# One bank of a first network layer set ahead of the second step's off-diagonal products

## The chip, the cores and the metric

The kernel runs on one core of a Trainium2 chip. The metric is the device time of one execution in microseconds (us). A core has a matrix engine (PE, with its weight loads shown apart as PEld), a vector engine (DVE), a scalar engine (ACT), a general engine (POOL) and a queue engine (SP) that here only issues DMAs. Each engine works through its own instructions in order and waits for the others by semaphores.

## What is computed

Two blocks in a row. The first is a linear attention with a forget gate; the second is a network with a per-feature leaky activation:

```python
# q, k, v, f_logit: (B=4, H=8, S=768, D=48), float32
f = 1.0 / (1.0 + np.exp(-f_logit))
for t in range(S):
    state = f[:, :, t, :, None] * state + np.einsum('bhd,bhe->bhde', k[:, :, t], v[:, :, t])
    y[:, :, t] = np.einsum('bhd,bhde->bhe', q[:, :, t], state)
x = y.transpose(0, 2, 1, 3).reshape(B * S, H * D)        # 3072 tokens x 384
h = x @ w_in                                              # 384 x 2048
g = np.maximum(h, 0.0) + alpha * np.minimum(h, 0.0)
return g @ w_out                                          # 2048 x 384
```

## The kernel before

**Steps.** The sequence is cut into 6 chunks of 128 tokens, and the batch into 2 pairs of sequences. One step is one chunk of one pair (256 tokens); there are 12 steps, and the two pairs alternate. The first two steps belong to the first chunk (c = 0), where there is no state yet to start from, and they take some paths of their own.

**What a step does.** Four generators write the instructions of a step; each `yield` ends a piece.
- `prepare` (letters P and Q) loads q, k, f and v, applies the sigmoid, and builds on DVE and ACT the scaled copies of q and k (`qd`, `us`, `q3`, `kh`, `ks`, `k4`) from scans of f. Its sixth and last piece copies parts of `q3` into the attention matrix `A` (L407, ACT).
- `carry` (O), first piece: PE computes the off-diagonal products `off` (L432, and for c = 0 also L442), ACT copies them into `ad` (L446) and `A` (L450); for c = 0 PE also transposes `ks` into `pk` (L459), and ACT copies that to `ksn` (L462). Second piece: PE multiplies `ksn` with v into `pd` (L472), which feeds the state kept beside v in `vs`.
- `attend` (S): for each of two sequences PE computes `raw` (L508) and `qu` (L523), and DVE moves the allowed entries into `ad` (L514, L545 for c = 0 or L529 else). Then ACT copies `ad` into `A` (L551), PE computes `py` from `vs` and `A` (L562), and the result is copied (L571) and turned into `xT`, the network's input: on PE in the first step (`xt`, L580, copied by L582), by DMAs in the others.
- `network` (n): in each of its first eight pieces PE fills one PSUM bank `ph` with two column tiles of x @ w_in (L606: 6 products of 128x128 by 256, which the trace shows as 12 MATMUL), ACT forms `neg` (L611), and DVE forms `gate` in two operations (L613). Then follows the second layer: in the first step 32 products into `po` (L626) over the whole of w_out, later a scheme with sums and fewer products (L645).

**Weights.** The weights arrive as 64-bit words and are converted by hand. For each of 8 pieces of w_in and 8 of w_out, ACT runs three operations (L201, L203, L204; letter a for w_in, b for w_out), and DVE a `lead` (L214) and a `both` (L219; letters w and v). The raw words have four buffers and are loaded by SP; the operations between ACT and DVE have three. A piece of w_in holds just the columns of one bank of the first step. Letter W closes this stage and forms differences of blocks of w_out on DVE (L706).

**PSUM.** `raw`, `qu`, `off`, `pk`, `pd` and `py` share one pool of two pairs of banks; `ph`, `xt` and `po` share a pool of four single banks. A tile waits until the earlier one in its place has been read.

**Order.** The order of PE, DVE and ACT is the order of the program, which is written out by hand as a string of letters for each step: a letter with a number takes that many pieces of that generator. In the string of step n, P, O and S stand for the pieces of step n, lower-case n for the network of step n - 1, and Q for `prepare` of step n + 1. The first four steps have strings of their own (`first`, L712), the others share `usual` (L718). So the string of the second step, which the change touches, holds the network of the first step, the `carry` and `attend` of the second, and the first five pieces of `prepare` of the third.

Of the kernel before, what the change touches and what calls it, by code (L numbers as in the profile page):

```python
# [31 lines left out]
def kernel(  # L32
# [39 lines left out]
    W = U * HP * C  # L72
# [66 lines left out]
    for m in range(1, NB):  # L139
        lo = UO[m] + (4 if m == 1 else 0)  # L140
        n = NB - m
# [4 lines left out]
    for half in range(2):  # L146
        for m in range(1, NQ):
            n = NQ - m
# [540 lines left out]
    def halves_of_w_out():  # L689
# [21 lines left out]
    steps = [(bp, c) for c in range(NC) for bp in range(B // U)]  # L711
    first = (  # L712
        "P5 a w P a2 O w S w a w a2 S Q S O S w Q2 S Q2 S w",
        "a2 w b w O w n2 b2 v S P v2 n2 S b v Q n b n O S2 v n b v n Q2 b v Q b n S v2 W Q W S n2 W n W",
        "n S P n2 S n W n O Q n3 O S Q n S Q n Q S2 Q n3",
        "S n3 P S Q S n O n O n4 Q S Q S Q n S Q n Q n2",
    )
# [81 lines left out]
```

## Time and profile before

| what | value |
|---|---|
| median of 3 runs | 625.14 us (624.67 to 626.03) |
| the profiled execution | 626.43 us, its span 624.6 us |
| mean granted clock of PE in the span | 0.995 |
| PE busy | 589.2 us, 94% of the span |
| DVE busy | 503.4 us, 81% |
| ACT busy | 260.5 us, 42% |
| POOL busy | 62.9 us, 10% |

The span runs from the first to the last instruction of the profiled execution; times within the trace count from its start. PE is busy 3.66 us from 40 to 45 us, 3.01 in the next five, 1.65 from 50 to 55 us, 4.53 from 55 to 60 us, and in nearly every window after it throughout. ACT is busy for most of the time up to 97 us and far less later. A timeline line gives start, duration, engine, source line, operation, output from inputs, shape and count; behind it in brackets stands the idle time of the engine before the group and what ended it. "issue" stands for a wait whose end the profile cannot name.

### The profile page before, as it was taken

The page shows a single profiled execution, that of the slowest core. Times are in us where ns is not written, and L with a number is a line of the kernel's source. Part 1 is how long each engine was busy: PE and PEld are TensorE (multiplying, and loading weights), DVE is VectorE, ACT ScalarE, POOL GpSimd, SP SyncE. Part 2 cuts the span into 40 slices and gives each one's busy share as a digit, 9 for nine tenths or more (in the row PEclk, how much of TensorE's full clock was granted, in tenths as well). Part 3 has the DMA queues.
Part 4 walks back from the last instruction along what each step waited for, and adds up shares of the span by engine and source line. Part 5 has one row for each costly group of instructions (what it writes and reads, how often), then busy time and mean ns, then how long its engine had stood idle before and what let it go on. Part 6 is the DMA issues. An engine that isn't in the chain of part 4 may idle for free.

```text
span 624.6 us, 19118 instructions
## 1 busy us (share of the span) xinstructions
PE 589.2 (94%) x8220; PEld 525.9 (84%) x8220; DVE 503.4 (81%) x1013; ACT 260.5 (42%) x482; POOL 62.9 (10%) x119
## 2 busy tenths in 40 slices
PE   3457999999999999999999999999999999999997
PEld 3346876789889889889889889889889889889997
DVE  7589989899799798889889888888888889762261
ACT  5797992261443252342343343243244244223110
POOL 9120010001001001001001001001001000000000
PEclk9998999899999999999999999999999999999999
DMA  9866513213314313413413313413314301201000
GB/s 298 278 225 196 200 41 93 75 35 86 87 36 90 82 35 86 87 35 85 87 35 85 75 49 85 83 38 87 73 49 85 68 22 26 53 3 26 26 0 26
DMA packets 68116, 50.43 MB, mean 81 GB/s; under 512 B 47168, under 2 KB 60608, under 8 KB 68032
## 3 DMA queue, kind: packets, MB, share of 16 engines
q1 hardware_dynamic: 56656, 25.01, 15.8%
q0 software_dynamic: 6864, 22.35, 12.6%
q10 hardware_dynamic: 4512, 1.85, 1.6%
q8 instruction: 65, 1.06, 0.8%
q14 instruction: 19, 0.16, 0.1%
HBM read 36.21 MB, written 4.72 MB: 66 GB/s over the span
## 4 chain that ended last, share of the span: by engine, by line
PE 60%; DVE 18%; ACT 16%; issue 4%; DMA 1%; ACTq 1%; DVEq 0%
PE ph L606 24%; PE pc L645 9%; PE pa L645 6%; PE pe L645 5%; PE pd L645 5%; ACT A L551 4%; ACT us L302 3%; DVE gate L613 3%; PE qu L523 3%; DVE S L687 3%; PE raw L508 3%; DVE qd L275 2%; PE py L562 2%; ACT neg L611 2%; PE pb L645 1%
## 5 line engine op out<-in xcount | busy, mean ns | idle before, releaser
L606 PE MATMUL ph<-xT,w_in_sb 128*128 128x256 f32 x1152 | 262.7, 385 | 0.0
L606 PEld LDWEIGHTS ph<-xT,w_in_sb 128*128 128x128 f32 x1152 | 216.8, 191 | 33.1 <-issue 2.6
L611 ACT ACTIVATE neg<-ph 128x512 f32<-128x512 f32 x96 | 57.1, 596 | 197.2 <-PE ph L606 156.1
L613 DVE SCALAR_TENSOR_TENSOR gate<-neg,om,ph 128x256 f32<-128x256 f32 x192 | 82.2, 478 | 50.3 <-ACT neg L611 50.2
L645 PE MATMUL pc<-t,S 128*128 128x192 f32 x352 | 61.7, 329 | 0.0
L645 PE MATMUL pa<-w_out_sb,gate 128*128 128x192 f32 x352 | 61.0, 327 | 0.0
L645 PEld LDWEIGHTS pa<-w_out_sb,gate 128*128 128x128 f32 x352 | 58.0, 190 | 0.6
L645 PEld LDWEIGHTS pc<-t,S 128*128 128x128 f32 x352 | 57.3, 190 | 0.6
L514 DVE COPY_PREDICATED ad<-mraw,raw 128x256 f32<-128x256 int32 (+1 forms) x96 | 42.4, 441 | 8.3 <-PE raw L508 5.8
L529 DVE COPY_PREDICATED ad<-mquad,qu 128x224 f32<-128x224 int32 (+6 forms) x140 | 41.9, 300 | 6.2
L407 ACT COPY A<-q 48x512 f32<-48x512 f32 x44 | 27.2, 617 | 37.4 <-DVE q L356 37.0
L551 ACT COPY A<-ad 32x256 f32<-32x256 f32 x96 | 38.6, 402 | 1.4
L318 DVE TENSOR_TENSOR us<-us,fs 128x768 f32<-128x768 f32 (+5 forms) x60 | 36.7, 612 | 0.0
L663 ACT COPY o<-pa 128x192 f32<-128x192 f32 x11 | 3.5, 318 | 75.3 <-PE pa L645 72.3
L562 PEld LDWEIGHTS py<-A,vs 128*64 128x64 f32 x768 | 25.7, 145 | 7.8 <-ACT A L551 3.3
L562 PE MATMUL py<-A,vs 128*64 128x64 f32 x768 | 28.7, 232 | 3.4 <-ACT A L551 1.4
L687 DVE TENSOR_TENSOR S<-gate 128x512 f32<-128x512 f32 x44 | 30.3, 688 | 0.8
L645 PE MATMUL pb<-t,gate 128*128 128x192 f32 x176 | 30.4, 326 | 0.0
L645 PE MATMUL pe<-w_out_sb,S 128*128 128x192 f32 x176 | 30.4, 326 | 0.0
L645 PE MATMUL pd<-w_out_sb,S 128*128 128x192 f32 x176 | 30.4, 326 | 0.0
L508 PEld LDWEIGHTS raw<-qd,k 48*32 48x32 f32 x1536 | 18.3, 109 | 14.0 <-issue 8.4
L508 PE MATMUL raw<-qd,k 48*32 48x80 f32 x1536 | 23.3, 243 | 6.8 <-ACT A L450 5.2
(109 smaller groups left out, 754.6 us busy)
## 6 DMA issues: line engine op xcount, KB each, us to landing
w_out_raw<-in_w_out SPq DMA_DIRECT2D x8, 767.8 KB, 4.4
w_in_raw<-in_w_in SPq DMA_DIRECT2D x8, 767.2 KB, 9.8
q<-in_qT POOLq DMA_DIRECT2D x11, 512.0 KB, 4.4
f<-in_fT POOLq DMA_DIRECT2D x11, 512.0 KB, 4.2
k<-in_kT POOLq DMA_DIRECT2D x11, 512.0 KB, 4.6
out<-o SPq DMA_DIRECT2D x24, 192.0 KB, 2.8
vs<-in_v POOLq DMA_DIRECT2D x22, 192.0 KB, 4.6
ksn<-kt SPq DMA_DIRECT2D x80, 32.0 KB, 2.0
```

Source lines behind the costliest of these rows:

```text
L318: nc.vector.tensor_tensor(us[:, :, UO[m]:UO[m] + 4 * n].rearrange("p g (i r) -> p g i r", r=4), us[:, :, skip:skip + 4 * n].rearrange("p g ...
L407: nc.scalar.copy(A[halves(cc)[1], :, par * HP:(par + 1) * HP, CH * cc:CH * (cc + 1)], q3[rows(par)].rearrange("p (u h c) s t -> p u h c (s ...
L508: nc.tensor.matmul(raw[DB * j:DB * (j + 1), par, hp * C:hp * C + QW], lhsT=k[r_, g * DB:(g + 1) * DB], rhs=qd[r_, g], start=True, stop=True)
L514: nc.vector.copy_predicated(adu[:, :, :, d:4], mraw[:, d, :, d:4].bitcast(I32).unsqueeze(1).broadcast_to((128, H, NB, n)), rv[:, :, QO[d]: ...
L529: nc.vector.copy_predicated(ad[:, u, :, :, 4 * m:DB], mquad[:, lo:lo + n].bitcast(I32).unsqueeze(1).unsqueeze(1).broadcast_to((128, 2, HP, ...
L551: nc.scalar.copy(A[s_, u, :, s_], ad[s_, u].rearrange("p r h t -> p (r h) t"))
L562: nc.tensor.matmul(py[64 * par:64 * par + 64, u, o:o + CH], lhsT=vs[bp][:, cc, u, hd * D:hd * D + 64], rhs=A[:, u, par * HP + hp, CH * cc: ...
L606: nc.tensor.matmul(ph[:, j * T:(j + 1) * T], lhsT=w_in_sb[:, kt, m * 128:(m + 1) * 128], rhs=xT[:, kt], start=(kt == 0 and j == 0), stop=( ...
L611: nc.scalar.activation(neg, phv, AF.Relu, scale=-1.0)
L613: nc.vector.scalar_tensor_tensor(gate[:, m % NH, m // NH], neg[:, j], om[:, m:m + 1], phv[:, j], ALU.mult, ALU.add)
L645: nc.tensor.matmul(to[:, 0:DH], lhsT=of(f), rhs=by(f), start=(f == 0 and not more), stop=(f == NH - 1), skip_group_check=True)
L687: nc.vector.tensor_tensor(to, x_, y_, op)
```

## The change

In the string of the second step, one of the two network pieces that stood together moves ahead of the O (the first piece of `carry` of the second step), behind the second w. Everything else stays.

```diff
     first = (
         "P5 a w P a2 O w S w a w a2 S Q S O S w Q2 S Q2 S w",
-        "a2 w b w O w n2 b2 v S P v2 n2 S b v Q n b n O S2 v n b v n Q2 b v Q b n S v2 W Q W S n2 W n W",
+        "a2 w b w n O w n b2 v S P v2 n2 S b v Q n b n O S2 v n b v n Q2 b v Q b n S v2 W Q W S n2 W n W",
```

On PE the first bank's 12 MATMUL now follow the `xt` products of the first step and precede `off` and `pk` of the second. On ACT its `neg` stands after the conversion of the first w_out piece and ahead of the copies L446, L450 and L462. On DVE its two `gate` operations stand ahead of the last `both` of w_in. The second bank keeps its place.

## The prediction

> **What bounds the kernel now.** I read the page first (PE busy 94% of the span), then windows of 10 us: PE is busy 9.7 us or more of every ten from 120 us to 620 us, so from there on PE sets the pace, and what is won before 120 us should arrive at the end. The change sits at 50 to 65 us. There, the timeline of PE (start, duration, engine, line; idle time before it in brackets):
>
> ```profile
> 46.97 2.83 PE L580 MATMUL xt<-y,dense 128*128 128x256 f32 x12 [1.79 <-ACT y L571]
> 51.59 0.75 PE L432 MATMUL off<-q,kh 48*32 48x32 f32 x64 [1.80 <-DVE q L356]
> 53.13 0.90 PE L442 MATMUL off<-us 48*32 48x16 f32 x86 [0.79 <-DVE us L392]
> 55.45 0.65 PE L442 MATMUL off<-us 48*32 48x16 f32 x42 [1.42 <-issue]
> 56.12 1.97 PE L459 MATMUL pk<-ident,ks 128*128 128x128 f32 x8
> 57.88 5.70 PE L606 MATMUL ph<-xT,w_in_sb 128*128 128x256 f32 x24
> 63.51 0.92 PE L508 MATMUL raw<-qd,k 48*32 48x80 f32 x64
> ```
>
> The reader is to see holes of 1.80, 0.79 and 1.42 us before 56 us, and the two banks (24 matmuls) only after them. The timeline of ACT shows who waits for the second bank:
>
> ```profile
> 58.48 0.92 ACT L204 ACTIVATE w_out_sb<-w_out_raw 128x768 int32<-128x768 uint32 x1
> 59.30 0.39 ACT L446 COPY ad<-off 128x128 f32<-128x128 f32 x2
> 59.60 1.26 ACT L450 COPY A<-off 32x256 f32<-32x256 f32 x4
> 60.89 1.07 ACT L462 COPY ksn<-pk 128x512 f32<-128x512 f32 x2
> 61.85 0.62 ACT L611 ACTIVATE neg<-ph 128x512 f32<-128x512 f32 x1
> 63.61 0.60 ACT L611 ACTIVATE neg<-ph 128x512 f32<-128x512 f32 x1 [1.15 <-PE ph L606]
> 64.11 1.01 ACT L201 ACTIVATE w_out_pos<-w_out_raw,bias 128x768 int16<-128x768 int16 x1
> ```
>
> After that 1.15 us ACT works without a gap over 0.3 us until 96.5 us, on the weights above all, so its start at 64.11 sets its end. DVE hangs on it, and PE on DVE:
>
> ```profile
> 87.02 0.56 DVE L214 TENSOR_TENSOR w_out_lead<-w_out_pos,w_out_neg 128x768 bf16<-128x768 bf16 x1 [1.02 <-ACT w_out_neg L203]
> ...
> 115.73 2.29 DVE L529 COPY_PREDICATED ad<-mquad,qu 128x224 f32<-128x224 int32 x7
> ```
> ```profile
> 118.17 1.07 PE L523 MATMUL qu<-us,k 48*32 48x112 f32 x64 [1.19 <-DVE ad L529]
> ```
>
> From 87.02 DVE has no gap up to 118.03, and the chain of waits runs the same way: ACT to 96, DVE from 100 to 118, then PE. In 56 to 116 us PE has almost no gap either, but it does not end last.
>
> **The change, part by part.** Nothing is removed or added: the bank's 12 matmuls and 12 weight loads, one `neg` on ACT and two `gate` operations on DVE move. The bank issues no DMA, and nothing on SP or POOL stands in another order.
>
> *PE.* A matmul of a bank takes 5.45/24 = 0.227 us (the undisturbed 24 at 65.08), a bank 2.73. The bank now follows `xt`, whose last product ends at 49.80; the last third needs the copy of `xT` at 49.83 + 0.37 = 50.20. If the first eight run before that it ends at 52.5, if all wait for it at 52.9. I take 52.7. What is queued behind it is `off`, which could go at 51.45 (DVE L356): it comes 1.1 us later. Its second group starts near 53.4 instead of 53.13. The hole before 55.45 has no named releaser: either it ends at a fixed time (then `pk` starts at 56.1 as before), or it moves with `off` (at most 1.1 us, `pk` at 57.2). With `pk` at its 1.97 the second bank ends at 60.9 to 62.0. Those who wait for `off` and `pk` are the copies of ACT, which reach them at 59.8 and 61.4; cover 2.5 us at the least, and without it the loss would be the 1.1.
>
> *ACT.* The moved `neg` stands now after the weights' conversion that ends at 59.3 and before the eight copies. Its step is 64.11 - 63.61 = 0.50 us. The bank was done 6 us earlier, so it does not wait. The copies slide by 0.50 and end at 62.35; the second `neg` follows at 62.35, with its bank done 0.4 to 1.5 us before. So the next conversion starts at 62.35 + 0.50 = 62.85 instead of 64.11: **1.26 us earlier**. The bounds are 0.9 (the later end of the bank, and its wake-up) and 1.35 (the short gap before the fourth `neg`, near 70.9, goes too).
>
> *What the sliding copies hold up.* `raw` takes the bank pair of `off`, free when L450 ends: 60.86 + 0.50 = 61.4; `qu` that of `pk`, 62.4. So PE stands idle up to 0.5 us before `raw` and a moment before `qu`, and the third and fourth banks start at 63.2 instead of 65.08: PE is 1.8 us ahead from there on. The fourth ends at 68.7; ACT wants it at 70.9 - 1.26 = 69.6. Cover 0.9 us.
>
> *DVE.* Its order gets two `gate`s (0.87) ahead of the last `both` of w_in: `neg` is ready at 59.9, DVE comes at 60.4, no wait. That `both` is 0.87 later; its piece is first read by the eighth bank near 81 us, so 18 us hide it. The second pair of `gate`s starts at 63.0 instead of 64.24, 1.24 earlier, and the rest of DVE follows in step with ACT (its idle 1.31 and 1.02 us at 84 and 87 are waits for ACT, which come earlier too). Loads: the weights' DMAs are released by ACT's conversions and move with them; the next steps' by PE and DVE.
>
> *Sum.* ACT, then DVE, then `qu` come 1.26 us earlier, at 116.9; PE is there 1.8 earlier and its wait grows from 1.19 to about 1.7. PE alone would give more, but DVE ends last. From 120 us PE carries 1.26 to the end. The profiled execution has 626.43 us (span 624.6, and 1.8 around it); 626.43 - 1.26 = 625.17. It lies 1.29 above the median of the runs, so I carry over the difference: 625.14 - 1.26 = **623.9**.
>
> *The clock.* Windows of 2 us (length, PE busy, granted clock, DMA, GB/s) show it halved twice in the span, both times after a stretch with holes and small products:
>
> ```profile
> 56.00:58.00 2.00, 1.99 (x16) 0.50 0.88 258
> ...
> 120.00:122.00 2.00, 2.00 (x5) 0.51 0.39 160
> 122.00:124.00 2.00, 2.00 (x7) 0.64 0.03 8
> ```
>
> The 24 matmuls at 119.17 took 7.40 us instead of 5.45: 1.95 lost on the path of the end. The change moves such stretches: it fills the first, opens one at 60.9 to 63.2, and makes the one before 119 longer (3.1 us from `raw` to `ph`, then about 3.7). What the clock does there the trace of before cannot say; bounded by the same row: 1.95 spared to 1.95 added. I take 0, since the second stretch was there and was charged already, and keep both ends.
>
> The Trainium skill ("TensorE: Matmul & The Clock Gate", Part 1 and "Why this matters for your kernels") says that the gate judges free-running windows of about 3.4 us and asks for no PE gap over some 3 us. Here a gap of 1.19 us among small products was enough for 3.4 us at half clock, so the measurement decides on the length of the gap. By the page's rule neither stretch would be charged and the sum would stay 1.26; by this trace the longer stretch speaks against the change, and free-running windows would make the charge vary from one execution to the next.
>
> **The rivals.**
> 1. *The clock spares time too.* With the half-clock stretch starting where PE still waits at 115 to 117, part of the 1.95 falls on idle time. For: `ph` now starts 1.26 earlier against the same window. Against: the stretch is longer. Price up to 1.95, I take half: 625.14 - 1.26 - 0.95 = 622.9.
> 2. *The gain is swallowed.* The new hole at 60.9 to 63.2 halves the clock for the third and fourth banks. They lose up to 1.95, the fourth ends at 70.65, and ACT waits for it where it stood before (70.5): 625.1, no change. For: 2.3 us of small products and waits there. Against: full banks on both sides.
> 3. *Slower: the longer wait before `qu` near 116 costs a half clock that the runs of the median did not have.* Price 1.95 against the gain of 1.26: 625.14 + 0.7 = 625.8; if the bank's gain goes as in rival 2 as well, 627.1. It decides when the stretch without full products passes from 3.1 us, charged perhaps only in some runs (the profiled one stands 1.29 above the median), to one that is always charged. Against: the profile has the charge already.
> 4. *The change does nothing*, if the bank could not start at 50 because its weights are not there. The first piece of w_in was finished at 24.6 and the bank's PSUM slot is long free: I give it nothing of its own.
>
> **How the numbers follow.** The forecast has 0.58, with 623.3 to 624.5 as its own range; rival 1 0.16, rival 2 0.12, rival 3 0.14. What a measurement can tell from no change is about 0.2%, 1.25 us, and the forecast stands just on that edge: I give half of it to faster (0.29) and half to within. Faster: 0.29 + 0.14 from rival 1 = 0.43. Slower: 0.09 from rival 3. The rest, 0.48, is within. The range must take in most of rivals 1 and 3: 622.3 to 626.0.
>
> **What would show it.** Right: a bank of 12 matmuls at 50 us ahead of `off`; no wait of ACT L611 before 63; the conversion after it near 62.9; the `qu` that waits for L529 near 116.9. Wrong: ACT idle before the first `off` copy at 59.8 (then `off` came too late); ACT waiting for the fourth bank near 70 (rival 2); DVE waiting between 87 and 118 for something else than ACT; a granted clock below 1 in more windows than these two (rival 3). If ACT's conversions come 1.2 us earlier and the end does not, the claim that PE only carries on from 120 us is wrong.

## The result and the profile after

The changed kernel takes 623.47 us (median of 20 runs, 622.71 to 626.52) against 625.12 us before (20 runs, 623.40 to 626.81): ratio 0.9977, 95% interval 0.9969 to 0.9986, or 1.65 us between the medians. The forecast was 623.9. The profiled executions stand at 625.07 (span 623.3) and 626.43: 1.36 apart, and both lie above their medians.

The timeline of PE in the changed kernel, the same stretch as before (start, duration, engine, line; idle time ahead of it in brackets):

```profile
46.82 4.72 PE L580 MATMUL xt<-y,dense 128*128 128x256 f32 x12 [1.68 <-ACT y L571]
51.37 2.75 PE L606 MATMUL ph<-xT,w_in_sb 128*128 128x256 f32 x12
54.06 0.76 PE L432 MATMUL off<-q,kh 48*32 48x32 f32 x64
...
56.23 1.09 PE L459 MATMUL pk<-ident,ks 128*128 128x128 f32 x8
57.16 2.76 PE L606 MATMUL ph<-xT,w_in_sb 128*128 128x256 f32 x12
61.72 0.92 PE L508 MATMUL raw<-qd,k 48*32 48x80 f32 x64 [1.80 <-ACT A L450]
```

The first bank stands ahead of `off`, `pk` starts about where it did (56.12 before), and the second bank ends at 59.9 instead of 63.6: one bank less stands there, 2.7 us, and `pk` took 1.09 us here, 1.97 before, where the granted clock read 0.50. PE then waits for ACT's copies. The timeline of ACT:

```profile
59.62 0.60 ACT L611 ACTIVATE neg<-ph 128x512 f32<-128x512 f32 x1
60.10 0.44 ACT L446 COPY ad<-off 128x128 f32<-128x128 f32 x2
...
62.65 0.61 ACT L611 ACTIVATE neg<-ph 128x512 f32<-128x512 f32 x1
63.14 1.01 ACT L201 ACTIVATE w_out_pos<-w_out_raw,bias 128x768 int16<-128x768 int16 x1
```

No wait before the second `neg`; the conversions behind it start 0.97 us earlier than in the first trace (64.11). And the end of the stretch, from the timelines of DVE and PE:

```profile
86.05 0.56 DVE L214 TENSOR_TENSOR w_out_lead<-w_out_pos,w_out_neg 128x768 bf16<-128x768 bf16 x1 [1.02 <-ACT w_out_neg L203]
...
114.77 2.30 DVE L529 COPY_PREDICATED ad<-mquad,qu 128x224 f32<-128x224 int32 x7
```
```profile
117.21 1.07 PE L523 MATMUL qu<-us,k 48*32 48x112 f32 x64 [1.36 <-DVE ad L529]
118.21 7.23 PE L606 MATMUL ph<-xT,w_in_sb 128*128 128x256 f32 x24
```

Everything is 0.96 us earlier, in step: 86.05 against 87.02, 114.77 against 115.73, 117.21 against 118.17. The half clock behind `qu` is there as before (7.23, before 7.40). What is new is `xt`: the same 12 matmuls took 4.72 us, before 2.83. So this one trace differs from the first by more than the change, and the experiments had to part the two.

### The profile page after: what moved, and what is told of

The parts are those of the page before. It is cut to its first block, busy times and chain, and to the rows that moved or that the text cites. A ratio compares the mean times of both kernels' runs of the same rounds, so it can differ in the third digit from the quotient of the medians.

```text
span 623.3 us, 19117 instructions
## 1 busy us (share of the span) xinstructions
PE 589.7 (95%) x8220; PEld 526.0 (84%) x8220; DVE 503.7 (81%) x1013; ACT 260.4 (42%) x482; POOL 62.7 (10%) x119
## 3 DMA queue, kind: packets, MB, share of 16 engines
HBM read 36.21 MB, written 4.72 MB: 66 GB/s over the span
## 4 chain that ended last, share of the span: by engine, by line
PE 58%; DVE 15%; ACT 12%; issue 3%; ACTq 0%; DMA 0%; DVEq 0%
PE ph L606 23%; PE pc L645 9%; PE pa L645 6%; PE pe L645 5%; PE pd L645 5%; ACT A L551 4%; DVE gate L613 3%; ACT us L302 3%; DVE S L687 3%; PE qu L523 3%; PE raw L508 2%; DVE qd L275 2%; PE py L562 2%; ACT neg L611 2%; PE pb L645 1%
## 5 line engine op out<-in xcount | busy, mean ns | idle before, releaser
L529 DVE COPY_PREDICATED ad<-mquad,qu 128x224 f32<-128x224 int32 (+6 forms) x140 | 42.0, 300 | 6.2
```

What stands on the lines that cost most here:

```text
L529: nc.vector.copy_predicated(ad[:, u, :, :, 4 * m:DB], mquad[:, lo:lo + n].bitcast(I32).unsqueeze(1).unsqueeze(1).broadcast_to((128, 2, HP, ...
```

## The experiments

The experiments were timed beside runs of the kernel before on the same chip, whose medians were 625.07 (e1 to e4, 35 runs), 625.29 (e5 to e8, 33) and 625.15 (e9 to e12, 21).

**e1, ACT's order alone.** The banks stay where they were; a conversion stands between the two `neg`s.

```diff
-        "a2 w b w O w n2 b2 v S P v2 ...
+        "a2 w b w O w n b n b v S P v2 ...
```

> The old order on PE: both banks stay behind off and pk. Only ACT is reordered: the next weight conversion (2.7 us) stands between the two negs, so that ACT no longer waits for the second bank. The theory (the gain is ACT's 1.15 us wait, handed on by DVE) expects the conversions behind it about 1.2 us earlier and about the gain of the change: 623.5 to 624.0 against 625.1. The rival that PE's work in its hole is what pays (2.7 us of matmuls taken out of the busy stretch) expects no gain, 625.1. The rival that the spared half clock pays expects 625.1 as well.

Measured: 624.72 us, ratio 0.9989 (0.9978 to 0.9999). Most of the gain is missing. The conversion did start at 62.42, but then the timelines of PE and ACT show:

```profile
56.97 7.03 PE L606 MATMUL ph<-xT,w_in_sb 128*128 128x256 f32 x24
...
65.36 5.45 PE L606 MATMUL ph<-xT,w_in_sb 128*128 128x256 f32 x24
```
```profile
69.25 0.59 ACT L611 ACTIVATE neg<-ph 128x512 f32<-128x512 f32 x1
70.90 0.60 ACT L611 ACTIVATE neg<-ph 128x512 f32<-128x512 f32 x1 [1.07 <-issue]
```

That last line is the `neg` of the fourth bank. PE ran `raw`, `qu` and these banks as late as before, and finished the fourth at 65.36 + 5.45 = 70.81; the 1.07 us end there, though the profile names no releaser. DVE L529 starts at 115.73, exactly as before. So ACT's wait was not the only thing that held the path; PE stood just behind it. PE was late by the clock here: the first two banks took 7.03 us, with the granted clock at 0.50 from 58 to 60 us. At the 5.45 us of the next two banks, the fourth would have ended near 69.2, ahead of ACT at about 69.7; this is an estimate, and no such execution of e1 was traced.

**e2, the hole filled without moving work.** The first bank is computed in the hole and again at its old place.

```diff
         for f in range(NH):
             ...
+            if plain and f == 0:
+                yield
+                for kt in range(NK):
+                    ...                      # the same products once more
-        "a2 w b w O w n2 b2 v S P v2 ...
+        "a2 w b w n O w n2 b2 v S P v2 ...
```

> The order of before, but the first bank is computed twice: once in the hole ahead of off, and again at its old place. PE has the hole filled and no work less afterwards. The rival of the clock expects the whole gain, 623.5. The rival of PE's work expects none, 625.1 or a little more. The theory of ACT's wait expects only what an earlier end of the second bank gives: off 1.1 us later, pk and the banks at full clock if the fill keeps it up, so the wait before the second neg shrinks from 1.15 to between 0.2 and 1.1 us: 624.2 to 625.1, and the shift of the conversions must equal the shift of the end.

Measured: 624.90 us, ratio 0.9991 (0.9979 to 1.0003), which is not told apart from no change. The runs fall into two groups, 623.08 to 623.62 (4 of 11) and 624.53 to 625.18 (7). The trace is one of the first group, with the full clock granted from 52 us to 120 us: there `pk` took 1.09, the conversions started at 62.76 and `qu` at 116.84. In lines, of PE and of ACT:

```profile
55.83 1.09 PE L459 MATMUL pk<-ident,ks 128*128 128x128 f32 x8
```
```profile
62.76 1.03 ACT L201 ACTIVATE w_out_pos<-w_out_raw,bias 128x768 int16<-128x768 int16 x1
```

So with 2.7 us more for PE to do, a full clock behind the hole alone was worth as much as the change, where it came about. This was the first sign that the clock on this stretch matters.

**e3, more work for ACT in the changed kernel.**

```diff
-            nc.scalar.activation(pos, top, AF.Relu, bias=bias[:, 0:1], scale=8.0)
+            for _ in range(3 if name == "w_out" and n == 1 else 1):
+                nc.scalar.activation(pos, top, AF.Relu, bias=bias[:, 0:1], scale=8.0)
```

> The changed kernel, with the first operation of the second w_out piece's conversion run three times instead of once: about 2 x 0.9 = 1.8 us more on ACT, right after the second neg; PE and DVE have the same work as in the changed kernel. The theory of ACT expects the whole 1.8 us at the end: 623.5 + 1.8 = 625.3, the gain gone. The rivals of PE's work and of the clock expect the gain to stay, 623.5, since ACT is busy 42% of the span.

Measured: 626.22 us, ratio 1.0022 (1.0010 to 1.0033). The edit adds a line, so L201 is L202 here:

```profile
62.81 3.06 ACT L202 ACTIVATE w_out_pos<-w_out_raw,bias 128x768 int16<-128x768 int16 x3
```

The three operations take 3.06 us, 2.05 more than the one of the changed kernel's first trace, and start 0.33 earlier (63.14 there), so ACT should be 1.72 us later behind them. `qu` starts at 118.92, 1.71 us later: the added work arrives there whole, though ACT is busy 42% of the span. The medians differ by more, 2.75 us; 5 of the 12 runs lie above 627, with a mean granted clock of 0.994 or 0.995. Why those are more frequent, and why even the three at 1.0 lie at 625.92 to 626.23, was not followed up.

**e4, one lead earlier on DVE.** The last `w` of the first string stands ahead of L482 and L486, to take away ACT's wait at 55.3.

```diff
-        "... O S w Q2 S Q2 S w",
+        "... O S w Q2 S Q2 w S",
```

> The changed kernel, and in the string of the first step the last w stands one piece earlier, ahead of the two state updates of DVE (L482, L486, 2.1 us). ACT waits there for this lead before the first w_out conversion (1.36 us before the change, 0 in the profile of the changed kernel, where xt was slow). The theory of ACT expects up to 1.2 us more where xt runs at full clock, and 0.3 to 0.8 where it does not: 622.3 to 623.2. The rival of PE's work expects no gain or a loss up to 1.5 us, since pk waits for L486, which comes 1.5 us later: 623.5 to 625.

Measured: 624.71 us, ratio 0.9994 (0.9983 to 1.0006): a loss of 1.2 us against the changed kernel, where the theory of ACT expected a gain and the rival up to this loss. The timeline of PE shows where it begins:

```profile
57.54 1.65 PE L459 MATMUL pk<-ident,ks 128*128 128x128 f32 x8 [1.35 <-DVE vs L486]
58.99 3.92 PE L606 MATMUL ph<-xT,w_in_sb 128*128 128x256 f32 x12
```

`pk` waits for L486, which was moved back. PE stands idle for 1.35 us more, the clock halves behind it, and the second bank ends at 62.9 instead of 59.9 (61.1 in e7 below, where the clock halves too). In this trace `qu` starts at 117.52, only 0.31 us later than in the changed kernel's first trace and 0.76 later than in e7, so it shows a part of the loss of the medians. This also answers what the prediction left open: `pk` starts near 56 in either order because L486 ends there (at 56.06 before, at 55.89 in the changed kernel's first trace), so the bank in the hole cost `pk` next to nothing.

**e5 and e6, the later wait filled in both kernels.** In the third step one bank is set between `raw` and `qu` of the second sequence, where PE waits for L529.

```diff
+            if (bp, c) == steps[2] and u == 1:
+                yield                        # between raw and qu
...
-        "n S P n2 S n W n O Q n3 ...
+        "n S P n2 S n S W n O Q n3 ...
```

> The changed kernel, and in the third step one network bank stands between raw and qu of the second sequence, where PE otherwise waits 1.2 to 1.4 us for DVE near 116 us and the clock then halves in many executions. If that wait and its half clock are on the path, the wait (1.36 us) is filled with work that has to be done anyway, and the 1.8 us of half clock behind it vanish: 621.5 to 622.5 against 623.5. If DVE is the bound after 118 us, nothing is won: 623.3.

> The kernel of before with the same edit in the third step. The difference between this and the changed kernel with the edit is what the change is worth where no half clock behind that wait can be charged. If the change's gain is the earlier handing on through ACT, DVE and PE, about 1.0 us of difference is left. If the gain is that fewer executions are charged the half clock near 119 us, the difference shrinks to 0.3 us or less, as the few executions without half-clock windows suggest (before 623.5 to 624.1, changed 623.2 to 623.7).

Measured: 623.26 us with the change (e5, ratio 0.9967, 0.9956 to 0.9979), 624.49 without it (e6, 0.9994, 0.9985 to 1.0004). The difference stays, 1.23 us, with neither the wait nor the half clock behind it in either trace (PE goes from `raw` to the bank to `qu` without a gap). As e6 expected for the theory of the path, about 1 us of difference is left; so the change does not live on fewer half clocks near 119 us. The edit itself brought little, 623.26 where 621.5 to 622.5 was expected if the wait were on the path: in e5 `off` of the third step comes at 122.38, against 123.51 in e7 below, yet the two traces stand at 623.46 and 623.40. In the new order the gates and sums of the bank stand ahead of the second L529 on DVE, which ends at 126.0 instead of 122.4; that DVE then holds the path is the likely reason, and was not tried by itself.

**e7, e9 and e10, more traces of the two kernels.** Unchanged code, other executions.

> The changed kernel once more, for a second trace and more times. The trace of the changed kernel has the half clock at 118 to 123 us and 625.07 us; most executions lie near 623.4. If the half clock near 119 us is what parts them, an execution near 623.4 shows 24 matmuls of ph behind the waiting qu in 5.45 us and not 7.23, and the same times up to there within 0.4 us.

> The kernel of before once more, for a second trace in another position of the clock's windows. Mechanism: the conversions after the second neg near 64.0 whatever the clock does to xt, since ACT waits there for the second bank; qu behind L529 near 118.1. The 24 matmuls behind it 5.5 to 5.8 us where the time is near 623.6 to 625.1, and 7.2 to 7.4 us where it is near 626.

> The kernel of before a third time, as the one ahead of it: the start of qu behind L529 is to stay within 0.4 us of 118.1 if the mechanism carries the gain, and the time is to follow the half clock behind it.

The changed kernel again: 623.73 us (12 runs, ratio 0.9979, 0.9968 to 0.9989). In its trace, of 623.40 us, `xt` runs as fast as in the first trace of before, and the half clock falls on nearly the same place (by the windows of 2 us from 55.2 to 58.6 us before, from 55.6 to 59.0 in e7), so these two can be laid side by side. Timelines of PE and ACT of e7:

```profile
55.98 1.97 PE L459 MATMUL pk<-ident,ks 128*128 128x128 f32 x8
57.75 3.39 PE L606 MATMUL ph<-xT,w_in_sb 128*128 128x256 f32 x12
...
63.09 5.45 PE L606 MATMUL ph<-xT,w_in_sb 128*128 128x256 f32 x24
...
116.76 1.07 PE L523 MATMUL qu<-us,k 48*32 48x112 f32 x64 [1.37 <-DVE ad L529]
117.76 5.82 PE L606 MATMUL ph<-xT,w_in_sb 128*128 128x256 f32 x24
```
```profile
62.18 0.62 ACT L611 ACTIVATE neg<-ph 128x512 f32<-128x512 f32 x1
62.67 1.02 ACT L201 ACTIVATE w_out_pos<-w_out_raw,bias 128x768 int16<-128x768 int16 x1
```

The conversions are 64.11 - 62.67 = 1.44 us earlier, `qu` 118.17 - 116.76 = 1.41. `xt` itself started 0.13 earlier in this trace (46.84, before 46.97), which leaves 1.31 and 1.28: the predicted 1.26. Expected were also 5.45 us for the 24 matmuls behind `qu` and a `qu` within 0.4 us of the first trace of the changed kernel; they took 5.82, and `qu` came 0.45 earlier, so both missed by a little.

The kernel before again, 625.31 (e9) and 626.77 us (e10), one run each. Here its timelines show the wait to be longer than in the first trace; e10, PE and then ACT:

```profile
56.30 1.97 PE L459 MATMUL pk<-ident,ks 128*128 128x128 f32 x8
58.06 7.33 PE L606 MATMUL ph<-xT,w_in_sb 128*128 128x256 f32 x24
```
```profile
62.83 0.60 ACT L611 ACTIVATE neg<-ph 128x512 f32<-128x512 f32 x1 [0.74 <-PE ph L606]
65.42 0.60 ACT L611 ACTIVATE neg<-ph 128x512 f32<-128x512 f32 x1 [1.99 <-PE ph L606]
```

The two banks took 7.33 us instead of 5.70, since two windows at half clock in a row followed the hole, and ACT waited 0.74 + 1.99 us instead of 1.15. In e9 it waited 1.59 us. Expected was `qu` within 0.4 us of 118.1; it came at 118.93 and 120.01, so that expectation missed, and the miss is the finding: the old order's path is exposed to the clock behind the hole. The conversions, expected near 64.0, came at 64.88 and 65.92. And e10 stands at 626.77 with only 5.82 us behind `qu`, where 7.2 to 7.4 were expected: its time comes from the late `qu`.

**e8, the bank moved on PE alone.** Its `neg` and `gate`s keep their old places.

```diff
+            if plain and f == 0:
+                yield                        # ahead of neg
...
-        "a2 w b w O w n2 b2 v S P v2 ...
+        "a2 w b w n O w n2 b2 v S P v2 ...
```

> The change on PE alone: the bank ahead of off and pk, but its neg stays behind the copies of off and pk on ACT, and its gates behind the last both on DVE. ACT has no wait before the second neg in this order either, so its conversions start as early as in the changed kernel, and the copies stand 0.5 us earlier, which frees the banks for raw earlier: 623.0 to 623.5, no slower than the change. If the order of the neg is what pays, 625.1.

Measured: 623.46 us, ratio 0.9975 (0.9965 to 0.9985): the whole gain. Within the interval it doesn't matter where the `neg` stands.

**e11, both banks ahead of `off`.** Against the changed kernel:

```diff
-        "a2 w b w n O w n b2 v S P v2 ...
+        "a2 w b w n2 O w b2 v S P v2 ...
```

> The changed kernel with the second bank ahead of off and pk as well: off comes 2.7 us later again, near 55 to 57 us, pk near 58 to 59. The copies of off on ACT stand behind two negs now, near 60.1 us, so off is still there in time, and ACT's conversions start as before. The theory of ACT and PE together expects no more gain, 623.3 to 623.9: the second bank was not waited for any more. The rival that any bank in the hole pays expects about 1.3 us more: 622.2.

Measured: 624.89 us, ratio 1.0000 (0.9988 to 1.0013): nothing is left of the gain, and both expectations missed. Timelines of PE and ACT:

```profile
61.69 1.34 PE L508 MATMUL raw<-qd,k 48*32 48x80 f32 x64 [4.05 <-ACT A L450]
...
63.80 6.68 PE L606 MATMUL ph<-xT,w_in_sb 128*128 128x256 f32 x24
```
```profile
68.94 0.59 ACT L611 ACTIVATE neg<-ph 128x512 f32<-128x512 f32 x1
70.57 0.60 ACT L611 ACTIVATE neg<-ph 128x512 f32<-128x512 f32 x1 [1.04 <-issue]
```

The second bank no longer fills the time while ACT copies. PE is idle for 4.05 us, the clock is halved from the idle stretch on (59.5 to 66.3 us), the third and fourth banks take 6.68 instead of 5.45, and ACT waits for the fourth again, as in e1. This is what rival 2 of the prediction described, in another kernel than the one predicted.

**e12, e8 and the edit of e5 together.** The diffs are those of e8 and e5.

> The bank ahead of off on PE with its neg and gates left where they were, and in the third step one bank between raw and qu: the two edits that were each no slower than the changed kernel. 622.9 to 623.5, the lower end if the wait before qu is partly on the path; 623.5 if DVE bounds all after 118 us.

Measured: 622.78 us, ratio 0.9961 (0.9948 to 0.9974), the lowest of all. It beats the kernel before; against the changed kernel the intervals overlap, and the two were not run together, so that it is the faster of them is likely but not shown.

**All traces of the unchanged third step side by side.** Times in us; "behind" is the duration of the 24 matmuls that follow `qu`.

| kernel | time of the trace | start of `qu` | behind | time less start |
|---|---|---|---|---|
| before | 626.43 | 118.17 | 7.40 | 508.3 |
| e9, before | 625.31 | 118.93 | 5.79 | 506.4 |
| e10, before | 626.77 | 120.01 | 5.82 | 506.8 |
| changed | 625.07 | 117.21 | 7.23 | 507.9 |
| e7, changed | 623.40 | 116.76 | 5.82 | 506.6 |
| e1, ACT alone | 624.72 | 118.18 | 5.83 | 506.5 |
| e2, filled | 623.08 | 116.84 | 5.45 | 506.2 |
| e3, more ACT | 625.66 | 118.92 | 5.82 | 506.7 |
| e4, lead early | 624.14 | 117.52 | 5.82 | 506.6 |
| e8, PE alone | 623.15 | 116.71 | 5.55 | 506.4 |
| e11, both ahead | 624.93 | 117.90 | 5.84 | 507.0 |

From the start of `qu` on, nine of them need 506.2 to 507.0 us, whatever was edited, and the two where the half clock follows 507.9 and 508.3. So the time of these executions is read from two places: when `qu` starts, and whether the clock is halved behind it.

**All runs by their mean granted clock.** One window of 3.4 us at half clock is worth 3.4 x 0.5 / 622 = 0.0027 of the mean, so 0.999 and 1.0 stand for none on record, 0.997 for one, 0.995 or less for two or more. The rows take in every run of before that was made beside the experiments or as e9 and e10, and all runs of the changed kernel; those at 0.978, where the clock record starts earlier, are left out. Chance and not an edit sorts the runs here, and where a window lay is known for the traced ones only.

| mean granted clock | before: runs, median | changed: runs, median |
|---|---|---|
| 0.999 and 1.0 | 12, 623.58 us | 4, 623.47 us |
| 0.997 | 24, 625.12 us | 22, 623.38 us |
| 0.995 and less | 45, 625.76 us | 2 (623.90 and 626.52) |

Without a half clock on record the two kernels are 0.1 us apart. With one window on record the old order is 1.5 us slower than with none, and the new order's median is no slower.

## Why the prediction was right, and where its sizes were off

*PE carries on from 120 us.* Shown by the table: what is won at `qu` arrives at the end.

*ACT's 1.26 us.* The mechanism and the size were right where the clock is alike (1.31 and 1.28 in e7). The reading "its start at 64.11 sets its end" was too simple. e1 gave ACT the early start and got almost nothing, since the fourth bank ended at 70.8. The step that made the change work is the one the prediction wrote as a side remark, "PE is 1.8 us ahead from there on", with a cover of 0.9 us at the fourth bank. In e7 that bank ends at 63.09 + 5.45 = 68.54 and ACT would need it near 69.4. Where the half clock falls on these banks, one bank fewer on PE's busy stretch and the lost wait of ACT are both needed, and moving the one bank gives both. In e2's trace, at full clock, the conversions started as early (62.76) with no bank fewer. PE's wait before the `qu` near 117 grew to 1.36 and 1.37 us, not to about 1.7.

*`off` and `pk` behind the bank.* Right, with cover to spare; of the two cases left open for the hole before 55.45 the first one held, as `pk` waits for L486 anyway (0.35 us in e9, 0.67 us in e6).

*DVE in step.* Right: 0.96 us at three places in the changed kernel's trace.

*The clock.* "I take 0" was the mis-sized term. The prediction looked at the stretch near 119 us and expected the surprise there; e5 and e6 show that the gain does not hang on it. The charge that the change takes off the path lies at 55 to 64 us: the half clock that follows the hole runs through `pk` and the two banks ACT waits for. The prediction took "`pk` at its 1.97" as the price of `pk`. At full clock it is 1.09 (e2), and the two banks are 5.45 instead of 5.70, so 0.88 + 0.25 = 1.13 us of ACT's wait of 1.15 were the half clock. The order alone left ACT almost nothing to wait for. This is an estimate, since no trace of the old order has a full clock there; the 12 runs of before without a half clock on record, with a median of 623.58, agree with it.

So the 1.26 us is not a gain to which the clock adds something: it is nearly all the price of the half clock in one execution. In others of the old order the wait was 1.35 (e6), 1.59 (e9) and 0.74 + 1.99 (e10). In the new order the same half clock falls on a bank with about 1 us to spare (e7: the second bank ends at 61.1, its `neg` starts at 62.18). That the medians are 1.65 apart and not 1.26 fits these larger charges. That the sum came near is partly luck with the first trace: an execution near 623.5 would likely have shown next to no wait to remove, and e10 one of 2.73 us.

*The rivals.* Rival 1 had the right sign and the wrong place. Rival 2 did not come true here; its whole chain decided e11, and its end, ACT waiting for the fourth bank, e1. Rival 3 did not: the changed kernel is charged near 119 us in some executions, as the one before is, and its few runs above 625 fit such a charge. How often either is charged there stays open, since only one trace of each set of runs can be looked into. Part of the 0.96 us of the first trace instead of 1.26 is the slow `xt`: the first w_out conversion started at 57.03 instead of 56.68, because the slow copies of `xT` used up ACT's wait of 1.36 us and 0.35 more.

## What to carry to other kernels

When an engine's wait is removed, look for the engine that was nearly as late: here, with the clock halved, the fourth bank ended at 70.53 before and ACT read it at about 70.9, so relieving ACT alone brought little. An idle stretch of the matrix engine can cost twice, once as a wait and again as half clock on what follows; ask of a wait in a trace how much of it is the clock, count the second cost on whatever the path waits for there, and fill such a stretch only as far as none opens behind it (one bank paid, two did not). Lay two traces side by side only after seeing that the clock fell on the same places in both.

## What the runs showed of the hardware

**The granted clock of a trace can be silent about its beginning.** In the changed kernel's first trace 12 matmuls of `xt` took 4.72 us (2.83 in e7), and the window around them still reads a granted clock of 1.00; e3, where it is recorded, reads 0.50 with 4.38 us. Columns: window, its length, PE busy, granted clock, DMA share, GB/s; first the changed kernel, then e3.

```profile
48.00:52.00 4.00, 4.00 (x14) 1.00 0.46 134
```
```profile
48.00:50.00 2.00, 2.00 (x7) 0.50 0.76 202
```

The likely reading is that the column shows 1.00 until its first recorded change, so until then a slow group of known size tells more. The mean clocks in the table of runs can miss such a start too. The executions with a mean clock of 0.978 are not slower for it (624.79 to 625.72 in the kernel before).

**The half clock moves from execution to execution of one kernel**, in windows of 3.4 us. In the first trace the rows from 120 us, at 0.51 and 0.64, make 1.96 + 1.44 = 3.4 us at half clock, and in e10 the stretch behind the hole is 6.8 us, two in a row. `xt` took 2.83 us in seven of the 14 traces and 4.38 to 5.46 in the other seven, and the pair of banks behind the hole between 5.70 and 7.33 in the four traces of the old order with a fast `xt`. The Trainium skill ("TensorE: Matmul & The Clock Gate", Part 1) says that the windows run freely and that where a matmul lands in them varies from run to run; these traces agree. It asks for idle gaps above some 3 us before the clock falls ("Why this matters for your kernels"); here, ahead of 55 us in the first trace, gaps of 0.79 to 1.80 us among small products were enough, and the measurement decides.
